# The last tile of a fused attention and two-MoE kernel: order of the gated half-groups on TensorE, and where the expert weights' conversions and the row-number copies stand on VectorE

## The chip, the cores and the metric

The kernel runs on one core of a Trainium2 chip. The metric is the device time of one execution in microseconds (us). The page of the profile and the trace come from one execution of the kernel taken by the hardware profiler; the times are those of runs of the same kernel.

## What is computed

Three layers follow one another. `q`, `k`, `v` are 2 x 8 x 576 x 64, so there are N = 1152 tokens of width 512.

```python
# attention with the 32 largest scores of each row kept
scores = q @ k.T / sqrt(64); kth = 32nd largest of the row
attn = softmax(where(scores >= kth, scores, -1e9)); x = attn @ v        # -> (1152, 512)
# first MoE layer: RMS norm, gate, value, output (d_ff = 1536)
xn = x / rms(x) * rms_g
g = xn @ w_gate;  x = (silu(g) * (xn @ w_val)) @ w_out
# second MoE layer: every token goes to the expert with the largest logit (8 experts, F = 1024)
e = argmax(x @ r_gate); gate = softmax(x @ r_gate)[e]
disp[e, counts[e]] = x[token]            # at most `capacity` = 288 tokens an expert
out[token] = gate * (relu(disp[e] @ w1[e]) @ w2[e])[pos]
```

## The kernel before

The tokens are cut into nine tiles of 128 (NT = 9, the last is tile 8). All products of the two MoE layers use numbers split into two 16-bit halves ("high" and "low"), so one product of float32 numbers is three matmuls: high x high, high x low, low x high.

**The first layer of a tile** is `moe1` (L479). The 1536 columns are worked on in three groups g = 0, 1, 2 of 512. A group has two half-groups, the gate (w = 0) and the value (w = 1), numbered b = 2g + w, so b runs from 0 to 5. A half-group is 12 matmuls (four chunks of the contraction by three) into one bank of PSUM (L500). After the gate half, ScalarE takes tanh (L507) and VectorE makes `th = (th + 1) * a` (L508); after the value half, VectorE makes `gs = a * vg * th` (L511). `turned` (L483) transposes the result with four TensorE transposes (L486), and `halves` (L469) splits it into `hT`: ScalarE copies the high half (L470), VectorE subtracts for the low one (L471). The output product is 36 matmuls, f = 0 to 11 by three (L528), which read `hT` of group f // 4; ScalarE evicts it as `yx` (L532).

For the last tile, four of the six half-groups write banks of the pool `late`, which has two buffers (`if late and b % 3`: b = 1, 2, 4, 5); b = 0 and 3 write a bank of `pm`. So b = 4 can only start when `gs` of group 0 has read b = 1.

**The dispatch of a tile** (L537 and following) transposes `yx` (L541), takes the router's logits (L555), splits the row into halves, finds the largest logit and the token's position, writes the slot (L616) and scatters the row with an indirect DMA issued by GpSimd to the buffer `disp` (L618). In the last tile its small steps are VectorE's; in the others many are GpSimd's. In the last tile's dispatch the first 128 tokens of expert 0 are fetched by a transposing DMA on SP (`gather("a", ...)`, L838), which waits for the scatter of tile 7; the remaining tokens of expert 0 come after the last scatter, by an indirect DMA on GpSimd into `xb` (L899) and a transposing DMA on SP into `xbT` (L903).

**The experts' weights** are 16 matrices of 2 MB in the order `ORDER = [0, 1, 2, 3, 4, 6, 5, ...]` (2e is w1 of expert e, 2e + 1 is w2). Each is loaded in two pieces on SP's queue (L776), `size` takes its sum of squares on ScalarE (L792) and works out a power of two as its scale in some small VectorE steps (L801 to L813, L148, L151) around a small TensorE sum (L803), and `convert` makes its halves. For the first four weights `convert` works in four pieces of 128 x 1024: high of pieces 0 and 1 on ScalarE (L822), high of pieces 2 and 3 on VectorE (L824), low of all four on VectorE (L827). The later ones are worked on in two pieces of 128 x 2048.

**The expert products** are `up` (L916 into `acc`; then L927 on ScalarE and L928 on VectorE make `hE`) and `down` (L916; then L936 on VectorE makes `yT`). "a" is the first 128 tokens of expert 0, "b" its other 48, then come experts 1 to 7 with room for 168 tokens each. `send` transposes, scales and scatters the result to the rows whose numbers `target` (L940) has copied into integers (L944 for "a" and "b", L948 for the others, L974 in `finish`).

**What sets the order.** The program is written as generators that are advanced by hand; each engine's queue is then put in order by the compiler's scheduler, which simulates the engines and takes instructions that are ready by priority. An engine runs its queue strictly in that order. `with after(t, name):` puts every instruction traced in the block behind the named one if both run on the same engine, and nothing else. Before the change such orders stand at these places: the first output matmuls of the last tile (f = 0, 1) behind the transposes of group 1, the others behind those of group 2 (L526); weight 0 and 1's conversion behind the split of `xn` of tile 8 ("xn"), weight 2's behind the split of the last tile's last `hT` ("dve"), and weight 3's behind the last tile's slot ("slot"):

```python
    with after(NT - 1, "xn"):
        convert(0, 0)
    size(2, 2)
    with after(NT - 1, "xn"):
        convert(1, 1)
    with after(NT - 1, "dve"):
        convert(2, 2)
    ...
    up("a", 0, WA, 2)
    with after(NT - 1, "slot"):
        convert(3, 3)
```

Of the kernel before, what the change touches and what calls it, by code (L numbers as in the profile page):

```python
# [62 lines left out]
def whole(  # L63
# [371 lines left out]
    def norm(t, ew):  # L435
# [30 lines left out]
        behind[t, "xn"] = halves(xnT[t], xn)  # L466
        yield

    def halves(out, x):  # L469
        nc.scalar.activation(out[:, :KC], x, AF.Copy)  # L470
        return nc.vector.tensor_tensor(out[:, KC:], x, out[:, :KC], op=OP.subtract)  # L471
# [7 lines left out]
    def moe1(t, ew):  # L479
# [10 lines left out]
        for g in range(3):  # L490
# [3 lines left out]
            for w in range(2):  # L494
                b = 2 * g + w
                a = late[0].tile([P, DM], F32, name="late") if late and b % 3 else pm.tile([P, DM], F32, name="pm")
                for c in range(KC):
                    i = KC * b + c
                    for n, (x, lo) in enumerate(((0, 0), (0, 1), (KC, 0))):
                        nc.tensor.matmul(a, xn[:, x + c, :], half(i, lo), start=(c == 0 and n == 0), stop=(c == KC - 1 and n == 2))  # L500
# [5 lines left out]
                if w == 0 and ew is nc.vector:  # L506
                    nc.scalar.activation(th, a, AF.Tanh, scale=gdec[:, g:g + 1])  # L507
                    nc.vector.scalar_tensor_tensor(th, th, 1.0, a, op0=OP.add, op1=OP.mult)  # L508
                elif ew is nc.vector:
                    h = mx.tile([P, DM], F32, name="x" if t == NT - 1 and g == 1 else "gs")  # L510
                    nc.vector.scalar_tensor_tensor(h, a, vg[:, g:g + 1], th, op0=OP.mult, op1=OP.mult)  # L511
# [10 lines left out]
        for f in range(NF1):  # L522
# [3 lines left out]
            with after(t, "turn", 1 if f < 2 else 2) if t == NT - 1 else nullcontext():  # L526
# [10 lines left out]
    def dispatch(t):  # L537
# [69 lines left out]
        ev.tensor_scalar(yd[:, DM:DM + 1], nm[:, 3:4], yn[:, 2:3], 1.0 / YS, op0=OP.mult, op1=OP.mult)  # L607
# [207 lines left out]
    def convert(j, n):  # L815

        raw, (hi, lo), sc = raw_of(n), place(j), sized.pop(j)
        k = 4 if n < 4 else 2
        for g in range(k):
# [5 lines left out]
        for g in range(k):  # L825
            r = slice(g * 2 * BIG // k, (g + 1) * 2 * BIG // k)
            nc.vector.scalar_tensor_tensor(lo[:, r], raw[:, r], sc[:, 7:8], hi[:, r], op0=OP.mult, op1=OP.subtract)  # L827
# [48 lines left out]
    with after(NT - 1, "xn"):  # L876
        convert(0, 0)
    size(2, 2)
    with after(NT - 1, "xn"):
        convert(1, 1)  # L880
    with after(NT - 1, "dve"):
        convert(2, 2)
# [47 lines left out]
    def down(k, e, n):  # L930
        yT2[k] = eb.tile([P, KC, n], F32, name="yT2", bufs=1)
        for lo, hi in groups(KC, n):
# [3 lines left out]
            nc.vector.tensor_scalar(yT2[k][:, lo:hi, :], a, es[e][:, 8:9], None, op0=OP.mult)  # L936
# [28 lines left out]
    def finish():  # L965
# [36 lines left out]
    with after(NT - 1, "slot"):  # L1002
        convert(3, 3)
# [118 lines left out]
```

## Time and profile before

| what | value |
|---|---|
| time of three runs | 668.9 us median (666.94 to 671.46) |
| the profiled execution's own time | 668.38 us |
| its span, from the first to the last instruction | 666.2 us |
| TensorE busy in the span | 588.6 us (88%) |
| VectorE busy | 542.3 us (81%) |
| ScalarE busy | 502.6 us (75%) |
| GpSimd busy | 350.4 us (53%) |
| mean granted TensorE clock | 0.976 of full speed |

PE is TensorE's matmuls, PEld its weight loads, DVE is VectorE, ACT ScalarE, POOL GpSimd, SP SyncE, which issues most DMAs; PEclk is the granted TensorE clock as a share of the full 2.4 GHz. Times in the trace count from the span's start. In a timeline a row is a run of like instructions: start, time covered, engine, line, operation, output and inputs, shape, count, and in brackets how long the engine was idle before it and what ended that. Attention and the first eight tiles fill the time to about 487 us, the last tile's first layer the time to about 523 us, its dispatch that to about 529 us, and the experts the rest.

### The profile page before, as it was taken

Reading aid. Unit: us, or ns where it says so; the run is one execution under the profiler, and the core shown is the slowest. Engines: PE = TensorE matmul, PEld = TensorE weight load, DVE = VectorE, ACT = ScalarE, POOL = GpSimd, SP = SyncE. Lnnn points to the kernel's source line nnn. Section 1 sums busy time; section 2 is a strip of 40 time slices with the busy share of each in tenths; the row PEclk is TensorE's granted clock in tenths of the full one; section 3 lists DMA queues with packets and bytes.
Section 4 is the critical chain, followed back from the end, with each engine's and each line's share of the span. In section 5 each row is a group of like instructions: output and inputs, shape, how many; then the busy total and the mean of one; then the engine's idle time right before and its main releaser. Section 6 shows DMA issues by size and latency. Waiting matters only on the chain. (4 is left out here: it accounts for less than half of the span.)

```text
span 666.2 us, 13476 instructions
## 1 busy us (share of the span) xinstructions
PE 588.6 (88%) x4817; PEld 412.8 (62%) x4817; DVE 542.3 (81%) x1495; ACT 502.6 (75%) x972; POOL 350.4 (53%) x490
## 2 busy tenths in 40 slices
PE   1417879789999999999999999999998879999995
PEld 1304455445666666666666666665544679999995
DVE  3979999978989979989988999861476867999951
ACT  3359979897787978878897988885697429899711
POOL 2476735636368879958788698683212100121412
PEclk9999979899999999999999999999998879999998
DMA  7988445923100010100000000007500589999001
GB/s 214 260 294 294 179 139 183 322 84 89 33 14 27 18 44 9 33 17 29 13 16 27 17 26 0 1 17 293 213 16 1 174 237 372 344 356 305 33 22 42
DMA packets 47006, 80.05 MB, mean 120 GB/s; under 512 B 18716, under 2 KB 23324, under 8 KB 46930
## 3 DMA queue, kind: packets, MB, share of 16 engines
q1 hardware_dynamic: 45138, 74.28, 35.2%
q0 software_dynamic: 1792, 4.83, 2.2%
q8 instruction: 39, 0.64, 0.4%
q14 instruction: 37, 0.30, 0.1%
HBM read 64.35 MB, written 12.27 MB: 115 GB/s over the span
## 5 line engine op out<-in xcount | busy, mean ns | idle before, releaser
L500 PE MATMUL pm<-wbig,xn 128*128 128x512 f16 x600 | 147.9, 381 | 0.5 <-DVE hT L471 0.5
L916 PEld LDWEIGHTS <-split 128*128 128x128 f16 x1728 | 117.4, 100 | 5.7 <-issue 5.6
L399 POOL TENSOR_TENSOR pp<-s,pp 128x576 f32<-128x576 f32 x72 | 102.3, 1436 | 21.5 <-ACT pp L398 21.1
L500 PEld LDWEIGHTS <-xn 128*128 128x128 f16 x648 | 62.7, 99 | 64.1 <-issue 5.3
L376 DVE MAX8 m<-r 128x8 f32<-128x288 f32 x216 | 96.4, 451 | 2.5
L373 DVE MATCH_REPLACE8 r<-m,r 128x288 f32<-128x288 f32 x216 | 95.0, 441 | 0.0
L317 PE MATMUL tp<-kst,qh 128*128 128x288 f32 (+1 forms) x160 | 64.4, 410 | 33.9 <-ACT s L319 16.8
L528 PE MATMUL pm<-wbig,hT 128*128 128x512 f16 x324 | 76.7, 380 | 0.0
L827 DVE SCALAR_TENSOR_TENSOR split<-raw,sc,split 128x2048 f16<-128x2048 f32 (+1 forms) x32 | 65.6, 2078 | 0.7 <-ACT split L822 0.7
L319 ACT ACTIVATE s<-tp 128x288 f32<-128x288 f32 x144 | 56.8, 417 | 10.7 <-PE tp L317 8.9
L317 PEld LDWEIGHTS tp<-kst,qh 128*128 128x128 f32 (+1 forms) x160 | 31.1, 195 | 53.0 <-ACT s L319 23.7
L423 ACT ACTIVATE pt<-tp 128x384 f32<-128x384 f32 x108 | 51.9, 500 | 15.6 <-PE tp L422 11.1
L916 PE MATMUL acc<-hE,split 128*128 128x168 f16 (+2 forms) x864 | 60.9, 233 | 2.5 <-DVE hE L928 2.2
L430 PE MATMUL xps<-pt,vt 128*64 128x128 f32 (+1 forms) x800 | 62.4, 275 | 0.0
L422 PE MATMUL tp<-ident,pp 128*128 128x128 f32 x324 | 58.0, 288 | 4.9 <-DVE r L325 2.6
L792 ACT ACTIVATE junk<-raw 128x2048 bf16<-128x2048 f32 (+1 forms) x32 | 54.1, 1691 | 8.2 <-DMA raw<-in_w_dram 6.4
L916 PE MATMUL acc<-xgT,split 128*128 128x168 f16 (+1 forms) x768 | 58.1, 238 | 2.3 <-DVE yT L936 1.5
L398 ACT ACTIVATE pp<-s,bias 128x576 f32<-128x576 f32 x72 | 52.2, 777 | 9.3 <-POOL bias L381 9.2
L404 ACT ACTIVATE pp<-pp,bias 128x576 f32<-128x576 f32 x72 | 57.0, 792 | 2.3 <-POOL pp L399 2.1
L422 PEld LDWEIGHTS tp<-ident,pp 128*128 128x128 f32 x324 | 40.3, 145 | 23.7 <-DVE r L325 3.4
L430 PEld LDWEIGHTS xps<-pt,vt 128*64 128x64 f32 x800 | 43.9, 138 | 13.7 <-issue 11.6
L528 PEld LDWEIGHTS <-hT 128*128 128x128 f16 x324 | 30.0, 98 | 32.0 <-issue 1.0
(241 smaller groups left out, 1226.5 us busy)
## 6 DMA issues: line engine op xcount, KB each, us to landing
raw<-in_w_dram SPq DMA_DIRECT2D x28, 1024.0 KB, 8.1
wbig<-in_w_gate_dram SPq DMA_DIRECT2D x6, 1024.0 KB, 9.0
wbig<-in_w_val_dram SPq DMA_DIRECT2D x6, 1024.0 KB, 9.8
wraw<-in_w_out_dram SPq DMA_DIRECT2D x12, 512.0 KB, 6.1
disp<-wraw SPq DMA_DIRECT2D x18, 257.0 KB, 5.5
qraw<-in_q_l_dram SPq DMA_DIRECT2D x72, 64.0 KB, 2.2
wbig<-in_k_l_dram SPq DMA_DIRECT2D x16, 288.0 KB, 4.0
split<-in_w_dram SPq DMA_DIRECT2D x4, 1024.0 KB, 7.6
```

Source lines behind the costliest of these rows:

```text
L317: nc.tensor.matmul(sp[:c1], x[:, i, :c1], kst[b, hp][:, i, c * HALF:(c + 1) * HALF], start=(n == 0), stop=(n == 1))
L319: nc.scalar.activation(s[:, c * HALF:(c + 1) * HALF], sp, AF.Copy)
L373: nc.vector.match_replace(h[i], to[n - 1][:, i], h[i], -3.0e38)
L376: nc.vector.max(to[n][:, i], h[i])
L399: nc.gpsimd.tensor_tensor(w, s[i], w, op=OP.subtract)
L404: nc.scalar.activation(pp[p][:, i], pp[p][:, i], AF.Exp, bias=bias[:, i, 0:1], scale=0.125, accum_out=sums[t][:, h:h + 1])
L422: nc.tensor.transpose(tp[:, i, :], p2[:, o:o + P], ident)
L430: nc.tensor.matmul(xps[t][rows, hp, c0:c1], v, w, start=(n == 0), stop=(n == 4))
L500: nc.tensor.matmul(a, xn[:, x + c, :], half(i, lo), start=(c == 0 and n == 0), stop=(c == KC - 1 and n == 2))
L528: nc.tensor.matmul(yps, hT[f // KC][:, KC * hi + f % KC, :], half(i, lo), start=(f == 0 and n == 0), stop=(f == NF1 - 1 and n == 2))
L827: nc.vector.scalar_tensor_tensor(lo[:, r], raw[:, r], sc[:, 7:8], hi[:, r], op0=OP.mult, op1=OP.subtract)
L916: nc.tensor.matmul(a, u[:, c, col * P:(col + 1) * P], v[:, c, :a.shape[-1]], start=(c == 0 and n == 0), stop=(c == nk - 1 and n == 2))
```

## The change

Five things are changed, all of them orders.

1. In the last tile, half-group b = 1 is put behind all products of b = 0, b = 3 behind all four transposes of group 0, b = 5 behind those of group 1. The output products f = 0, 1 stand behind b = 5 instead of behind group 1's transposes.
2. `convert` can be called for its high halves and for some of its low pieces alone.
3. Weight 1: high, and low of pieces 0 and 1, as before; low of 2 and 3 behind `gs` of group 0. Weight 2: high behind `th` of group 1 (its ScalarE part behind that group's tanh), low of 0 and 1 behind `gs` of group 1, low of 2 and 3 behind the last `hT` split ("dve").
4. Weight 3: high, and low of 0 and 1, behind "dve" (ScalarE: behind tanh of group 2) instead of behind the slot; low of 2 and 3 stay behind the slot (and behind the gate value written in the dispatch).
5. The row-number copies (L944, L948, L974) are put behind the `yT` of the same part ("a", "b"), those of the other experts behind the `yT` of "b".

Weight 0's conversion is also put behind the ScalarE half of the `xn` split; it stood behind it already.

```diff
@@ moe1
+                ahead_of = (None, ("prod", 0), None, ("turn", 0), None, ("turn", 1))[b] if t == NT - 1 else None
...
-                    for n, (x, lo) in enumerate(((0, 0), (0, 1), (KC, 0))):
-                        nc.tensor.matmul(a, xn[:, x + c, :], half(i, lo), start=(c == 0 and n == 0), stop=(c == KC - 1 and n == 2))
+                    with after(t, *ahead_of) if ahead_of else nullcontext():
+                        for n, (x, lo) in enumerate(((0, 0), (0, 1), (KC, 0))):
+                            behind[t, "prod", b] = nc.tensor.matmul(
+                                a, xn[:, x + c, :], half(i, lo), start=(c == 0 and n == 0), stop=(c == KC - 1 and n == 2))
...
-            with after(t, "turn", 1 if f < 2 else 2) if t == NT - 1 else nullcontext():
+            with after(t, *(("prod", 5) if f < 2 else ("turn", 2))) if t == NT - 1 else nullcontext():
@@ convert
-    def convert(j, n):
+    def convert(j, n, high=True, low=range(4)):
...
-        for g in range(k):
+        for g in range(k) if high else ():
...
-        for g in range(k):
+        for g in low[:k]:
@@ the calls
-    with after(NT - 1, "xn"):
+    with after(NT - 1, "xn"), after(NT - 1, "xn high"):
         convert(0, 0)
     size(2, 2)
     with after(NT - 1, "xn"):
-        convert(1, 1)
+        convert(1, 1, True, (0, 1))
+    with after(NT - 1, "gs", 0):
+        convert(1, 1, False, (2, 3))
+    with after(NT - 1, "th", 1), after(NT - 1, "tanh", 1):
+        convert(2, 2, True, ())
+    with after(NT - 1, "gs", 1):
+        convert(2, 2, False, (0, 1))
     with after(NT - 1, "dve"):
-        convert(2, 2)
+        convert(2, 2, False, (2, 3))
...
-    with after(NT - 1, "slot"):
-        convert(3, 3)
+    with after(NT - 1, "dve"), after(NT - 1, "tanh", 2):
+        convert(3, 3, True, (0, 1))
+    with after(NT - 1, "slot"), after(NT - 1, "gate"):
+        convert(3, 3, False, (2, 3))
@@ target, finish
-            nc.vector.tensor_copy(to[:m], meta[k, i][:m, 1:2])
+            with after(k, "down"):
+                nc.vector.tensor_copy(to[:m], meta[k, i][:m, 1:2])
...
-            nc.vector.tensor_copy(targets[i][:m, 1:], every[i][:m, 1:, 1])
+            with after("b", "down"):
+                nc.vector.tensor_copy(targets[i][:m, 1:], every[i][:m, 1:, 1])
...
-            nc.vector.tensor_copy(to[:m], every[i][:m, k, 1:2])
+            with after("b", "down"):
+                nc.vector.tensor_copy(to[:m], every[i][:m, k, 1:2])
```

## Rows read from the trace of the kernel before

**Rows 1.** Busy time by stretch: engines, PEclk, DMA share, GB/s.
```profile
487.00:498.10 11.10, 11.10 (x63) 5.38 (x61) 9.86 (x23) 11.01 (x20) 0.69 (x2) 1.00 0.00 0
498.10:501.65 3.55, 0.23 (x7) 0.16 (x5) 3.55 (x7) 3.55 (x7) 0.43 (x1) 1.00 0.01 2
501.65:505.40 3.75, 3.75 (x12) 1.86 (x12) 3.58 (x11) 3.72 (x8) 0.00 (x0) 0.54 0.01 4
...
515.65:522.80 7.15, 7.10 (x34) 3.27 (x34) 5.86 (x7) 0.61 (x2) 1.36 (x2) 1.00 0.40 83
...
527.94:533.60 5.66, 5.66 (x75) 5.66 (x75) 5.62 (x14) 4.33 (x5) 1.98 (x3) 0.70 0.18 67
533.60:538.80 5.20, 1.69 (x19) 1.34 (x17) 2.88 (x9) 0.60 (x1) 1.06 (x1) 0.72 0.88 149
...
555.00:640.00 85.00, 82.96 (x1195) 82.17 (x1193) 82.28 (x132) 71.86 (x77) 15.54 (x9) 1.00 0.80 252
```

**Rows 2.** Timeline of PE in the last tile's first layer.
```profile
487.08 0.59 PE L500 MATMUL pm<-wbig,xn 128*128 128x512 f16 x2
...
493.98 3.83 PE L500 MATMUL late<-wbig,xn 128*128 128x512 f16 x17
...
501.65 1.33 PE L500 MATMUL late<-wbig,xn 128*128 128x512 f16 x3 [3.32 <-DVE gs L511]
...
515.65 0.63 PE L486 MATMUL pm<-ident,gs 128*128 128x128 f32 x4 [1.26 <-DVE gs L511]
516.11 6.64 PE L528 MATMUL pm<-wbig,hT 128*128 128x512 f16 x30
```

**Rows 3.** Timeline of DVE in the last tile.
```profile
497.80 0.68 DVE L508 SCALAR_TENSOR_TENSOR th<-th,pm 128x512 f32<-128x512 f32 x1
498.40 2.47 DVE L827 SCALAR_TENSOR_TENSOR split<-split,sc,split 128x1024 f16<-128x1024 f32 x2
...
500.85 0.74 DVE L511 SCALAR_TENSOR_TENSOR gs<-late,st,th 128x512 f32<-128x512 f32 x1
...
517.55 1.41 DVE L824 TENSOR_SCALAR split<-raw,sc 128x1024 f16<-128x1024 f32 x2
518.87 4.87 DVE L827 SCALAR_TENSOR_TENSOR split<-raw,sc,split 128x1024 f16<-128x1024 f32 x4
...
524.26 0.15 DVE L562 TENSOR_SCALAR yn<-yn 128x1 f32<-128x1 f32 x1 [0.46 <-ACT th L549]
```

**Rows 4.** Timeline of ACT: the tanh of the last tile's group 1.
```profile
502.81 0.67 ACT L507 ACTIVATE th<-late,st 128x512 f32<-128x512 f32 x1
```

**Rows 5.** Timelines of PE, DVE, ACT and SP around the last slot; last row: landing of xbT.
```profile
524.02 1.50 PE L916 MATMUL acc<-xgT,split 128*128 128x128 f16 x24
...
538.79 6.67 PE L916 MATMUL acc<-hE,split 128*128 128x128 f16 x83 [1.77 <-DVE hE L928]
...
528.63 0.27 DVE L616 TENSOR_SCALAR slot<-pos 128x1 int32<-128x1 f32 x1
...
530.14 4.87 DVE L827 SCALAR_TENSOR_TENSOR split<-raw,sc,split 128x1024 f16<-128x1024 f32 x4
...
538.00 0.14 DVE L944 CAST to<-xb 48x1 int32<-48x1 f32 x1 [2.31 <-DMA xb<-disp,rest]
...
531.72 0.58 ACT L927 ACTIVATE hE<-acc 128x512 f16<-128x512 f32 x1
...
537.99 1.19 SPq L903 DMA_TRANSPOSE xbT<-xb  x1
...
DMA to landing us min/median/max: 2.7/2.7/2.7
```

**Rows 6.** Timelines of POOL and SP: the scatters of tiles 7 and 8, gather "a".
```profile
515.39 1.12 POOL L618 DMA_INDIRECT disp<-yd,slot  x1 [0.33 <-POOL slot L616]
...
529.77 1.39 POOL L618 DMA_INDIRECT disp<-yd,slot  x1 [1.40 <-ACT junk L792]
...
518.45 1.36 SPq L838 DMA_TRANSPOSE xgT<-disp  x1
```

More of the change, by code (lines that the diff above doesn't have):

```diff
@@ L465, in norm, with halves @@
             nc.tensor.transpose(xn[:, c, :], sq[:, c * P:(c + 1) * P], ident)
-        behind[t, "xn"] = halves(xnT[t], xn)
+        behind[t, "xn"] = halves(xnT[t], xn, t, "xn high")
         yield
-    def halves(out, x):
-        nc.scalar.activation(out[:, :KC], x, AF.Copy)
+    def halves(out, x, *what):
+        behind[what] = nc.scalar.activation(out[:, :KC], x, AF.Copy)
         return nc.vector.tensor_tensor(out[:, KC:], x, out[:, :KC], op=OP.subtract)
@@ L506, in moe1 @@
                 if w == 0 and ew is nc.vector:
-                    nc.scalar.activation(th, a, AF.Tanh, scale=gdec[:, g:g + 1])
-                    nc.vector.scalar_tensor_tensor(th, th, 1.0, a, op0=OP.add, op1=OP.mult)
+                    behind[t, "tanh", g] = nc.scalar.activation(th, a, AF.Tanh, scale=gdec[:, g:g + 1])
+                    behind[t, "th", g] = nc.vector.scalar_tensor_tensor(th, th, 1.0, a, op0=OP.add, op1=OP.mult)
                 elif ew is nc.vector:
                     h = mx.tile([P, DM], F32, name="x" if t == NT - 1 and g == 1 else "gs")
-                    nc.vector.scalar_tensor_tensor(h, a, vg[:, g:g + 1], th, op0=OP.mult, op1=OP.mult)
+                    behind[t, "gs", g] = nc.vector.scalar_tensor_tensor(h, a, vg[:, g:g + 1], th, op0=OP.mult, op1=OP.mult)
                 elif w == 0:
@@ L606, in dispatch @@
         ev.tensor_scalar(pos[:, 2:3], pos[:, 0:1], float(cap), NOWHERE, op0=OP.is_ge, op1=OP.mult)
-        ev.tensor_scalar(yd[:, DM:DM + 1], nm[:, 3:4], yn[:, 2:3], 1.0 / YS, op0=OP.mult, op1=OP.mult)
+        behind[t, "gate"] = ev.tensor_scalar(yd[:, DM:DM + 1], nm[:, 3:4], yn[:, 2:3], 1.0 / YS, op0=OP.mult, op1=OP.mult)
         yield
@@ L813, in scale @@
             nc.vector.tensor_tensor(es[e][:, 8:9], es[e][:, 4:5], sc[:, 4:5], op=OP.mult)
-    def convert(j, n):
-        raw, (hi, lo), sc = raw_of(n), place(j), sized.pop(j)
+    def convert(j, n, high=True, low=range(4)):
+        raw, (hi, lo), sc = raw_of(n), place(j), sized[j]
         k = 4 if n < 4 else 2
-        for g in range(k):
+        for g in range(k) if high else ():
             r = slice(g * 2 * BIG // k, (g + 1) * 2 * BIG // k)
@@ L935, in down @@
                 product(a[:, c - lo, :], place(2 * e + 1), hE[k], NF2, DM, c)
-            nc.vector.tensor_scalar(yT2[k][:, lo:hi, :], a, es[e][:, 8:9], None, op0=OP.mult)
+            behind[k, "down"] = nc.vector.tensor_scalar(yT2[k][:, lo:hi, :], a, es[e][:, 8:9], None, op0=OP.mult)
     targets = {}
```

## The prediction

> **What bounds the kernel now.** I read first the busy time by stretch, to find where TensorE stands idle or runs slowly, then the timelines of the four engines there, to find who was late.
>
> The busy times show two regimes. Over the experts, from 555 to 640 us, TensorE is busy for 82.96 of 85 us and VectorE for 82.28 [rows 1]: two engines without room, so that stage is moved as a whole by what happens before it, and neither can run ahead of the other for long. The last tile is different. TensorE is full up to 498.1 us, then does 0.23 us of work in 3.55 us, and then runs for 3.75 us at a granted clock of 0.54, the lower of its two levels for nearly all of it [rows 1]. A second hole of 1.26 us stands before the last four transposes [rows 2]. After the last slot it happens a third time: in the 5.2 us from 533.6 TensorE works 1.69, so 3.51 are lost, at a clock of 0.72 [rows 1].
>
> Who was late is read from the brackets. Both holes of the tile wait for `gs` (L511) [rows 2]. VectorE was not waiting for data in front of the first: `th` ends at 498.48, two low pieces of weight 1 follow (2.47 us), and only then comes `gs`, at 500.85 [rows 3], though TensorE had written its input by 495.1 (17 products from 493.98, the first five of b = 1, at 0.215 us; the rate is 30 products in 6.64 - 0.19 us) [rows 2]. The hole after the slot has two owners: weight 3's conversion, whose low pieces hold VectorE from 530.14 to 535.01, and the row-number copy of "b", which stops VectorE 2.31 us for a DMA, with the second `hE` behind it [rows 5].
>
> **The change part by part.**
>
> *Half-groups in turn.* No matmul is added. The first thirteen places of the tile now alternate b = 0 and b = 1; given to b = 0 alone, its twelve end near 487.08 + 12 x 0.215 = 489.7 instead of 494.0 [rows 2]. So tanh and `th` can come up to 4 us earlier, between weight 0's pieces, and `gs` may stand where `th` stood, at 497.8 [rows 3]; its input is there since 495.1. It then ends near 498.5, and TensorE's hole shrinks from 3.32 to about 0.5. With so short a hole I take the clock as not falling: after the hole of 1.26 us the row from 515.65 shows 1.00 [rows 1]. That gives back 3.75 x (1 - 0.54) = 1.7 us too. Recoverable, with the second hole, is 3.32 + 1.7 + 1.26 = 6.3 us.
>
> I don't take all of it, since a new wait appears. TensorE, from 498.6, has four transposes (0.45), b = 3 and b = 4 (24 x 0.215 = 5.2) before group 1's transposes, so it gets there soon after 504. These need `gs` of group 1, hence tanh of group 1, which ScalarE does at 502.81 [rows 4]; ScalarE is full (11.01 of 11.10 us [rows 1]) and the change takes nothing from it before that. Then `th` (0.68), the two high pieces of weight 2 that are now allowed behind it (1.41) and `gs` (0.75) follow, with hand-overs: near 507.0. Then 0.45 of transposes and b = 5 (2.6) to 510.0, f = 0, 1 (1.3) to 511.3, while `gs` of group 2 needs about 0.95 after b = 5: no hole. The last transposes start near 511.3 instead of 515.65 [rows 2]: **4.3 us earlier**, so 2.0 of the 6.3 are given back. Below, if `gs` keeps its place behind weight 1's pieces, only the second hole and some of the slow stretch go (1.7); above, nothing is given back (6.3).
>
> *Conversions between the gates.* VectorE gets no more work in sum. Behind "dve" it had 1.41 + 4.87 = 6.28 us of weight 2 [rows 3]; it will have 2.47 of weight 2 and 1.41 + 2.47 of weight 3, 6.35. This lies beside the 30 output products (6.64) and was over just before the dispatch's first step at 524.26 [rows 3]: I cost it at nothing. Without that cover it would be late by what is left of it. On ScalarE the two high pieces of weight 3 fall into a stretch in which it works 0.61 of 7.15 us [rows 1].
>
> *After the slot.* There VectorE had 6.3 us of weight 3 and now has 2.47, so from 528.9 it is free near 531.4. The first high `hE` is ready at 531.72 + 0.58 [rows 5], so the first low one ends near 533, and the second near 535. TensorE, which comes to `down("a")` at 533.6, then finds 12 products and hardly a hole (0.4). Of the 3.51 us lost, 3.1 return. The clock is 0.70 from 527.94 and 0.72 from 533.6 [rows 1]; without the hole `down("a")` should run nearer full speed. Its 83 products take 6.67 us, 0.080 each, against 0.0625 in the row of like ones from 524.02 (24 in 1.50) [rows 5]: worth up to 1.4. So `down("a")` would end 4.5 earlier than now, at 541.0 instead of 545.5, all before the shift of the tile is counted; `up("b")` needs `xbT`, issued at 537.99 with 2.7 to landing [rows 5], so 540.7: just there. That lead is no gain in time yet: VectorE is busy 82.28 of the 85 us that follow [rows 1] and has 2.7 us of holes to catch up with, and TensorE's own queue holds the sums for the weights' scales (L803), which need VectorE's steps first. The ends are 0 and 4.5; I take the middle, **2.2 us**, which lies within what VectorE's holes allow.
>
> *The copies behind `yT`* cost nothing: the scatters that need them come after the eviction of the same part's results.
>
> *Sum.* 4.3 + 2.2 = 6.5 us. The profiled execution took 668.38 (span 666.2, and 2.2 around it), 0.5 below the median of the runs: 668.4 - 6.5 = **661.9 us**.
>
> **The rivals.**
>
> *Stall kept (22%).* VectorE's order is made by a scheduler that had two low pieces between `th` and `gs` [rows 3] although the input was there; `convert(1)` keeps those two pieces free to stay in front. Then 1.7 + 2.2 = 3.9: 664.5. Against it: `th` itself moves up.
>
> *Nothing passed on after the slot (12%).* VectorE sets the pace over the experts and the TensorE lead is waited away: 668.4 - 4.3 = 664.1. For it speaks 82.28 of 85.
>
> *Slower (11%).* Weight 3's pieces, now free before the slot, are put between the small dependent steps of the last dispatch, which the scheduler does elsewhere (the pieces between `th` and `gs`). Six pieces are at hand, 6.35 us. If all land there, the slot (528.63 [rows 5]) is late by 6.3; with the first stall kept (1.7) the sum is +4.6, less 2.2 later: 668.4 + 2.4 = 670.8. It turns slower than before once more than 3.9 us of them stand in that chain. Against it: weight 2's 6.28 us ended before 524.26 in the same place.
>
> *Everything (9%).* Nothing is given back and the experts take the whole lead: 6.3 + 4.5 = 10.8: 657.6.
>
> *Tile 7's scatter late (6%).* Its steps on GpSimd now run beside conversions on VectorE. Gather "a" waits for this scatter (518.45), and TensorE uses it at 524.02 [rows 5, 6], in front of the dispatch's logits; the cover is at most 5.57 - 2.7 = 2.9 (by the landing of `xbT`), say 1.5. Three steps held by a piece of 1.22 each would be 3.7, so 2.2 too late: 668.4 - 4.3 = 664.1.
>
> On this the last scatter's row speaks: it took 1.39 us where tile 7's took 1.12 [rows 6], and high pieces of weight 3 ran on VectorE beside it. The Trainium skill (SBUF — State Buffer, "Who interferes with whom") says that the two engines share a port pair, that a scaling of this kind holds it for the whole instruction and that an instruction with two SBUF inputs holds off GpSimd's reads. The longer scatter agrees. By that rule tile 7's routing would meet the pieces now placed there and this rival would be likelier; the row alone shows 0.27 us.
>
> **How the numbers follow.** The forecast has 40%. About what a measurement can tell from no change is 1%, here 6.7 us, so faster means below 662.2 and slower above 675.6. The forecast lies just inside the first, so some six tenths of its share count there (24), with all of "everything" (9) and a part of the three near 664 (10): 0.43. Slower by over 1% needs all of the slow rival and more: 0.05. The rest, 0.52, is within. The range 657 to 668.5 takes in the forecast, the three at 664 and half of the upper end; it leaves out most of the slow rival.
>
> **What would show it.** Right: tanh of group 0 before 493 us; no hole over 1 us at the first group's transposes, and a clock of 1.00 there; a hole of about 2 us before group 1's transposes; the last transposes near 511.3; the slot near 524.3; no hole over 0.5 us at the start of `down("a")`; VectorE as full as before over the experts. Wrong: two low pieces still in front of `gs`, a conversion inside the dispatch's chain, or a TensorE wait for the scale sums (L803) that takes back the lead.

## The result, and the profile after

| | before | after |
|---|---|---|
| time, median of seven runs each on one chip | 669.5 us (666.94 to 671.46) | 662.4 us (660.06 to 663.67) |
| ratio, with its 95% interval | | 0.990 (0.987 to 0.992) |
| the profiled execution's own time | 668.38 us | 663.15 us |
| its span | 666.2 us | 661.2 us |
| mean granted TensorE clock | 0.976 | 0.976 |

The forecast of 661.9 us is 0.5 from the median. The time was right; of the two terms that made it, one came to half of its size, the other to nothing, and a third that I had not named made up for them. That their sum came out so near the forecast is luck. The rest of the document is about that.

Of the 5.2 us between the two profiled executions, 2.4 lie ahead of the last tile: its first product starts at 487.08 before and at 484.72 after. In both kernels the instructions of each engine stand in the same order up to there, and in the profiles of this study that start lies anywhere from 482.8 to 487.1. So times in the tile are compared from its own first product, and I call that t0.

Line numbers from L500 to L822 have moved by two or three and those from L916 by nine to eleven: L502 is the half-groups' products, L510, L511 and L514 tanh, `th` and `gs`, L531 the output products, L806 the scale sums, L825, L827 and L830 the conversions (high on ScalarE, high on VectorE, low), L925 the experts' products, L936 and L937 `hE`, L945 `yT`. In the kernels of the experiments the lines from L916 on differ from these by a few more.

The busy time by stretch, as in [rows 1], for the kernel after:

```profile
core 0: us, PE busy (x) PEld busy (x) DVE busy (x) ACT busy (x) POOL busy (x), PEclk, DMA share, GB/s
484.70:495.80 11.10, 11.10 (x62) 5.44 (x61) 9.97 (x23) 11.04 (x21) 0.90 (x2) 1.00 0.00 0
495.80:499.30 3.50, 3.50 (x24) 1.88 (x23) 3.50 (x9) 3.50 (x5) 0.05 (x1) 1.00 0.02 5
499.30:503.00 3.70, 3.09 (x19) 1.91 (x17) 3.70 (x7) 3.70 (x9) 0.00 (x0) 1.00 0.00 0
503.00:510.80 7.80, 5.43 (x33) 3.08 (x34) 7.80 (x22) 4.11 (x10) 3.47 (x5) 0.98 0.04 6
510.80:518.90 8.10, 8.06 (x30) 3.10 (x28) 7.35 (x13) 2.72 (x4) 3.92 (x5) 0.81 0.54 190
...
549.80:554.40 4.60, 4.53 (x112) 4.50 (x112) 4.23 (x15) 4.60 (x6) 0.00 (x0) 0.68 1.04 415
...
555.00:640.00 85.00, 83.77 (x1144) 83.20 (x1142) 81.18 (x133) 70.89 (x77) 16.72 (x10) 1.00 0.74 237
```

The second row answers to the hole of [rows 1]: TensorE worked 0.23 of 3.55 us there and now works all of 3.50, and the stretch at 0.54 behind it is gone. But the fourth row has 2.37 idle us in 7.80, the fifth runs at 0.81, and near 550 there is a stretch at 0.68 that the kernel before doesn't have. Where the idle time went is read from the brackets of the timelines. TensorE after, against [rows 2]:

```profile
496.36 0.60 PE L486 MATMUL pm<-ident,gs 128*128 128x128 f32 x4
...
503.55 0.66 PE L486 MATMUL pm<-ident,x 128*128 128x128 f32 x4 [1.16 <-DVE x L514]
...
510.04 0.72 PE L486 MATMUL pm<-ident,gs 128*128 128x128 f32 x4 [1.82 <-DVE gs L514]
510.55 8.31 PE L531 MATMUL pm<-wbig,hT 128*128 128x512 f16 x30
...
531.26 4.79 PE L925 MATMUL acc<-hE,split 128*128 128x128 f16 x83 [0.51 <-DVE hE L937]
537.74 2.60 PE L925 MATMUL acc<-xbT,split 128*128 128x48 f16 x96 [1.68 <-DMA xbT<-xb]
...
549.87 0.19 PE L806 MATMUL st<-s,ones 128*128 128x1 bf16 x2 [2.94 <-DVE s L804]
```

The first group's transposes wait for nothing. Those of group 1 wait 1.16, those of group 2 wait 1.82 (1.26 in [rows 2]), and the 30 output products behind them take 8.31 us instead of 6.64, in this execution. In the other two profiles of the changed kernel they take 6.64. In the second profile TensorE ran slowly earlier, behind the wait of 1.16, and so met the last `gs` without a hole. In all three the last transposes start 25.3 us after t0: it is `gs` that sets their time. VectorE after, against [rows 3], tells why:

```profile
493.96 0.75 DVE L514 SCALAR_TENSOR_TENSOR gs<-late,st,th 128x512 f32<-128x512 f32 x1
...
496.54 2.46 DVE L830 SCALAR_TENSOR_TENSOR split<-split,sc,split 128x1024 f16<-128x1024 f32 x2
...
499.05 2.46 DVE L830 SCALAR_TENSOR_TENSOR split<-split,sc,split 128x1024 f16<-128x1024 f32 x2
...
501.50 0.67 DVE L511 SCALAR_TENSOR_TENSOR th<-th,late 128x512 f32<-128x512 f32 x1
...
503.81 1.08 DVE L588 SCALAR_TENSOR_TENSOR key<-lg,m,rank 128x8 f32<-128x8 f32 x1
...
506.86 2.46 DVE L830 SCALAR_TENSOR_TENSOR split<-raw,sc,split 128x1024 f16<-128x1024 f32 x2
509.25 0.73 DVE L514 SCALAR_TENSOR_TENSOR gs<-late,st,th 128x512 f32<-128x512 f32 x1
...
512.03 1.28 DVE L830 SCALAR_TENSOR_TENSOR split<-raw,sc,split 128x1024 f16<-128x1024 f32 x1
...
513.29 1.27 DVE L830 SCALAR_TENSOR_TENSOR split<-raw,sc,split 128x1024 f16<-128x1024 f32 x1
...
549.65 0.17 DVE L804 CAST s<-sc 128x2 bf16<-128x2 f32 x1 [8.20 <-ACT junk L795]
```

Group 0 has its `gs` before any piece of weight 1. Group 1's `th` stands behind two low pieces of weight 1 (499.05), group 2's `gs` behind two low pieces of weight 2 (506.86). The stall of the kernel before has not left; it has gone two groups on.

To see where the time comes from over all profiles I cut each into four stretches at marks that every trace has: t0, the last four transposes of `moe1` (L486), the last slot (L619), the first product of the third expert, and the last matmul's end. For the kernel before these are 487.08, 515.65, 528.63, 557.65 and 659.33, for the changed one 484.72, 510.04, 524.74, 554.36 and 654.61. The differences, in us:

| kernel | t0 to last transposes | to the slot | to the third expert | to the end |
|---|---|---|---|---|
| before, two profiles | 28.57, 28.57 | 12.98, 12.98 | 29.02, 29.24 | 101.68, 104.34 |
| after, three profiles | 25.32, 25.34, 25.33 | 14.70, 13.66, 13.56 | 29.62, 29.31, 28.98 | 100.25, 99.50, 100.62 |
| order alone | 23.36 | 12.99 | 32.33 | 100.39 |
| conversions alone | 23.55 | 17.48 | 29.44 | 99.77 |
| copies alone | 27.40 | 12.99 | 32.24 | 101.04 |
| order, weight 1, copies | 23.36 | 12.99 | 31.70 | 102.43 |
| after, weight 2's low pieces later | 23.37 | 17.98 | 26.60 | 101.98 |
| after, sixth weight loaded early | 25.32 | 15.80 | 28.97 | 101.88 |

Some expectations below name 22.6 us to the last transposes, or 40.6 us to the slot. They count the order alone and the kernel with weight 2's pieces later from the tile's fourth product, 0.75 us behind the first; the table counts every kernel from its first.

In the mean over the profiles of each, the tile with its dispatch (the first two columns) gives 41.55 - 39.30 = 2.2 us, the way from the slot to the third expert gives nothing (29.13 against 29.30), and the rest of the experts gives 103.0 - 100.1 = 2.9. Together that is 5.0. The medians are 7.1 apart; the profiled executions of before took 668.38 and 667.45 us, both under their median of 669.5, which is most of the rest.

### The profile page after: what moved, and what is told of

The parts are those of the page before. It is cut to its first block, busy times and chain, and to the rows that moved or that the text cites. A ratio compares the mean times of both kernels' runs of the same rounds, so it can differ in the third digit from the quotient of the medians.

```text
span 661.2 us, 13479 instructions
## 1 busy us (share of the span) xinstructions
PE 588.5 (89%) x4817; PEld 412.1 (62%) x4817; DVE 540.5 (82%) x1495; ACT 502.3 (76%) x972; POOL 353.8 (54%) x490
## 4 chain that ended last, share of the span: by engine, by line
PE 52%; DVE 17%; ACT 9%; DMA 8%; POOL 6%; issue 6%; SPq 1%; POOLq 0%; DVEq 0%; ACTq 0%
PE pm L502 15%; PE pm L531 9%; PE acc L925 7%; PE xps L430 6%; PE tp L317 5%; PE tp L422 4%; DVE split L830 3%; DMA vt<-in_v_l_dram 3%; DMA raw<-in_w_dram 3%; ACT junk L795 2%; DVE r L373 2%; DVE wbig L169 2%; DVE wbig L168 2%; PE pm L486 2%; DVE split L827 2%
## 5 line engine op out<-in xcount | busy, mean ns | idle before, releaser
L502 PE MATMUL pm<-wbig,xn 128*128 128x512 f16 x600 | 145.7, 379 | 0.5 <-DVE hT L471 0.5
L925 PEld LDWEIGHTS <-split 128*128 128x128 f16 x1728 | 116.4, 99 | 4.3 <-issue 2.0
L502 PEld LDWEIGHTS <-xn 128*128 128x128 f16 x648 | 62.3, 98 | 60.2 <-issue 0.9
L531 PE MATMUL pm<-wbig,hT 128*128 128x512 f16 x324 | 78.4, 386 | 0.0
L830 DVE SCALAR_TENSOR_TENSOR split<-raw,sc,split 128x2048 f16<-128x2048 f32 (+1 forms) x32 | 65.9, 2077 | 0.5 <-ACT split L825 0.5
L925 PE MATMUL acc<-hE,split 128*128 128x168 f16 (+2 forms) x864 | 59.9, 231 | 1.7 <-DVE hE L937 1.7
L925 PE MATMUL acc<-xgT,split 128*128 128x168 f16 (+1 forms) x768 | 58.0, 239 | 0.0
L531 PEld LDWEIGHTS <-hT 128*128 128x128 f16 x324 | 30.4, 99 | 33.5 <-issue 2.7
```

The source lines that it names most:

```text
L502: behind[t, "prod", b] = nc.tensor.matmul(a, xn[:, x + c, :], half(i, lo), start=(c == 0 and n == 0), stop=(c == KC - 1 and n == 2))
L531: nc.tensor.matmul(yps, hT[f // KC][:, KC * hi + f % KC, :], half(i, lo), start=(f == 0 and n == 0), stop=(f == NF1 - 1 and n == 2))
L925: nc.tensor.matmul(a, u[:, c, col * P:(col + 1) * P], v[:, c, :a.shape[-1]], start=(c == 0 and n == 0), stop=(c == nk - 1 and n == 2))
```

## The experiments

Each kernel was compared with the kernel before on the same chip.

**1. The parts one by one, and the two kernels again.** For the order alone the calls of `convert` and the copies are put back:

```diff
-        convert(1, 1, True, (0, 1))
-    with after(NT - 1, "gs", 0):
-        convert(1, 1, False, (2, 3))
-    with after(NT - 1, "th", 1), after(NT - 1, "tanh", 1):
-        convert(2, 2, True, ())
-    with after(NT - 1, "gs", 1):
-        convert(2, 2, False, (0, 1))
+        convert(1, 1)
     with after(NT - 1, "dve"):
-        convert(2, 2, False, (2, 3))
+        convert(2, 2)
...
-    with after(NT - 1, "dve"), after(NT - 1, "tanh", 2):
-        convert(3, 3, True, (0, 1))
-    with after(NT - 1, "slot"), after(NT - 1, "gate"):
-        convert(3, 3, False, (2, 3))
+    with after(NT - 1, "slot"):
+        convert(3, 3)
```

For the conversions alone, the order (`ahead_of = None`, and f = 0, 1 behind the transposes of group 1 again) and the copies are put back; for the copies alone, the order and the conversions.

Order alone:

> Only part 1: the half-groups in turn, transposes in fours, f = 0, 1 behind b = 5. Conversions and copies as before. Theory T (the tile's gain is what reaches the end; the lead made after the slot is waited away at the weights' scale sums): gs of group 0 comes ahead of weight 1's low pieces, no hole over 1 us before group 0's transposes, none before the last transposes either since no low piece of weight 2 stands in front of gs of group 2, slot 4 to 6 us earlier counted from the tile's first matmul; the holes after the slot stay (3.5 us); ratio 0.991 to 0.995, so 663.5 to 666. Rival R (what counts is the room after the slot): the ratio is 0.996 to 1.000.

Conversions alone:

> Only parts 2 to 4: the weights' pieces placed around the gates and half of weight 3 ahead of the slot; half-groups and copies as before. Theory T: the first hole shrinks by the 2.5 us of the two low pieces that no longer stand in front of gs of group 0, conversions now stand in the last dispatch or in front of gs of group 2 and give some of it back; slot 0 to 3 us earlier; after the slot the row-number copy still stops VectorE for about 2 us; ratio 0.995 to 1.000. Rival R (room after the slot is what counts): 0.990 to 0.994.

Copies alone:

> Only part 5: the row-number copies behind the yT of the same part; everything else as before. Theory T: the second hE no longer waits for the DMA of xb, the TensorE hole of 1.8 us in down(a) goes, the lead of 2 us is waited away before 560 us: ratio 0.997 to 1.000. Rival R (the lead is kept): 0.995 to 0.997, about 2 to 3 us.

The changed kernel, and the kernel before, once more:

> The changed kernel once more, for a second profile. The first one began its last tile 2.4 us earlier than the kernel before although every queue is the same up to there. If that is the run and not the change, the start of the last tile here lies 0 to 3 us away from 484.7 and the distance from the tile's first matmul to the slot is 40.0 +- 0.3 (41.5 before), and the ratio is again 0.987 to 0.992. If it is the change, the last tile begins at 484.7 +- 0.5 again.

> The kernel before once more, for a second profile of it. Its first profile began the last tile at 487.1, the five other profiles between 483.6 and 486.5 although the queues up to there are the same. If that spread is the execution's and not the kernel's, the tile begins here anywhere from 483 to 487, the distance from its first matmul to the slot is 41.5 +- 0.5, and that from the first matmul to the last transposed result (172.3 before) is 171 to 174.

| kernel | median | ratio, interval |
|---|---|---|
| order alone | 663.96 us | 0.9934 (0.9911 to 0.9957) |
| conversions alone | 663.53 us | 0.9924 (0.9897 to 0.9951) |
| copies alone | 667.76 us | 0.9993 (0.9975 to 1.0012) |
| the changed kernel again | 661.34 us | 0.9907 (0.9874 to 0.994) |

The single run of the kernel before took 667.45 us. The order and the conversions are each worth about 0.7% by themselves, the copies nothing that can be measured. Added they would be 1.4%; the whole change gives 0.9 to 1.2% in its three measurements. With the intervals of these ratios that difference is not clear of noise, but the traces show that the two parts fill the same idle time: up to the last transposes the order alone gains 28.57 - 23.36 = 5.2 us and the conversions alone 28.57 - 23.55 = 5.0, of the 6.3 that the prediction called recoverable there. The order alone, TensorE at its first product, then VectorE, then TensorE:

```profile
482.81 0.81 PE L502 MATMUL pm<-wbig,xn 128*128 128x512 f16 x3
```

```profile
492.06 0.75 DVE L514 SCALAR_TENSOR_TENSOR gs<-late,st,th 128x512 f32<-128x512 f32 x1
...
494.63 2.46 DVE L830 SCALAR_TENSOR_TENSOR split<-split,sc,split 128x1024 f16<-128x1024 f32 x2
```

```profile
506.17 0.64 PE L486 MATMUL pm<-ident,gs 128*128 128x128 f32 x4
506.64 6.64 PE L531 MATMUL pm<-wbig,hT 128*128 128x512 f16 x30
...
545.07 0.19 PE L806 MATMUL st<-s,ones 128*128 128x1 bf16 x2 [4.68 <-DVE s L804]
```

With weight 1's conversion where it always was, `gs` of group 0 still goes ahead of its low pieces: the order of the products is enough for that. No piece of weight 2 stands in front of the last `gs`, the last transposes have no bracket, the output products take 6.64 again, and the slot is 36.35 us after t0, 5.20 earlier than before. Then more than half of it goes: TensorE waits 4.68 us for a scale sum, and the stretch to the third expert is 3.2 longer than before.

With the conversions alone the tile is quick too, 23.55 to the last transposes, but the dispatch takes 17.48 instead of 12.98. Up to the third expert this profile gains next to nothing, 70.47 us from t0 against 70.57 and 70.79 before. What the conversions gain in the median is not in these stretches; it may lie in the last one, which single profiles can't settle. GpSimd in that kernel, and below it TensorE:

```profile
512.63 1.28 POOL L620 TENSOR_TENSOR cum<-cum,oh 128x8 bf16<-128x8 bf16 x1 [0.90 <-PE px L599]
...
515.62 1.42 POOL L619 TENSOR_SCALAR slot<-pos 128x1 int32<-128x1 f32 x1
517.33 1.93 POOL L621 DMA_INDIRECT disp<-yd,slot  x1 [0.29 <-POOL slot L619]
```

```profile
524.34 2.72 PE L925 MATMUL acc<-xgT,split 128*128 128x128 f16 x24 [3.16 <-DMA xgT<-disp]
```

These are the routing steps and the scatter of tile 7. In the kernel before the same three took 0.20, 0.38 and 1.12 us; here pieces of the conversions run on VectorE beside them: two low ones from 512.59, two high ones from 515.59, two low ones from 516.99 to 519.46. The step at 515.62 ends at 517.04, the high pieces beside it at 517.01. The scatter is late, so gather "a" is late, and TensorE stands 3.16 us at the two columns of `up("a")`, which are in its queue in front of the last dispatch's sums. This is the rival to which I gave 6%. In the changed kernel the wait is there in small or not at all (0.80, 0.70, none), where the order has brought the scatter forward: it starts 27.5 us after t0 instead of 30.8.

**2. The sixth weight's load.** The scale sum that stops TensorE belongs to the second matrix of the third expert. SP issues its load only behind the last gathers. In the changed kernel, SP and then ScalarE:

```profile
536.14 1.46 SPq L841 DMA_TRANSPOSE xgT<-disp  x1
537.71 12.36 SPq L779 DMA_DIRECT2D raw<-in_w_dram  x8
```

```profile
543.76 1.91 ACT L795 ACTIVATE junk<-raw 128x2048 bf16<-128x2048 f32 x1 [2.90 <-DMA raw<-in_w_dram]
...
547.61 1.91 ACT L795 ACTIVATE junk<-raw 128x2048 bf16<-128x2048 f32 x1 [1.28 <-DMA raw<-in_w_dram]
```

The load is issued at 537.71, lands in two pieces 6.0 and 9.9 us later, ScalarE squares them, and VectorE, idle for 8.20 us, makes `s` at 549.65. To try whether this is what holds TensorE, the load goes ahead of the gathers, in the changed kernel and in one with the order and the copies alone:

```diff
+    fetch_w()
     last = gather(1, 1, 0, W, eb, nc.sync)
     rest_gather()
...
-        for _ in range(3):
+        for _ in range(2):
             fetch_w()
```

> The changed kernel with one more edit: the sixth weight (number 5 in the order of loading) is fetched ahead of the gathers of experts 1 to 3 on SP's queue, behind the conversion of weight 3 that frees its buffer, instead of behind them. Theory S (the lead of some 4 us that TensorE has after down(a) is lost because TensorE's queue holds the sum for this weight's scale, and the weight's load is issued only behind the last gather): TensorE's hole of 2.8 us before that sum goes, up(2) starts 3 us or more earlier counted from the tile's first matmul, VectorE uses its idle 8 us before it, and 2 to 4 us of it reach the end: ratio 0.984 to 0.988. Rival V (VectorE, busy 97% over the experts, sets the pace): the hole goes and others of the same sum come behind it; ratio 0.988 to 0.991, as the changed kernel.

> Parts 1 and 5 of the change and the early fetch of weight 5; weights 1 to 3 are converted as before the change (weight 2 behind the last hT, weight 3 behind the slot). Theory S: order alone brought the slot 6 us earlier and lost most of it at a hole of 4.7 us before the scale's sum; with the load early this hole shrinks to under 1.5 and the ratio is 0.981 to 0.987. Rival V: VectorE has half of weight 3 more to do behind the slot, so nothing is won on the changed kernel: 0.988 to 0.993.

Measured: 665.01 us, 0.9949 (0.9917 to 0.998), and 665.82 us, 0.9939 (0.9918 to 0.996), both by their medians slower than the changed kernel. The wait for the scale sum goes, and others come. TensorE in the changed kernel with the early load:

```profile
540.38 2.60 PE L925 MATMUL acc<-xbT,split 128*128 128x48 f16 x96 [2.55 <-DMA xbT<-xb]
...
552.41 0.19 PE L806 MATMUL st<-s,ones 128*128 128x1 bf16 x2 [0.67 <-DVE s L804]
```

2.94 has become 0.67, but `xbT` is waited for 2.55, where the three profiles of the changed kernel have 1.68, 1.38 and 1.37: SP issues its gather 12.0 us after the slot instead of 9.2 to 9.6. With the order and the copies that wait is 1.72, where the order alone has 0.41. The load was the cause of the wait for the scale sum, as expected; that moving it would pay was wrong. The weight and the gathers share SP's queue and the same stretch, and in these runs whichever was first made the other late. Gather "a" is waited for 1.06 us, little more than the 0.80 and 0.70 that the changed kernel has without the early load, but behind it TensorE ran at a granted clock of 0.51 for 6.17 us, and the slot came 15.80 us after the last transposes.

**3. Weight 2's low pieces out of the last gate's way.**

```diff
-    with after(NT - 1, "gs", 1):
+    with after(NT - 1, "gs", 2):
         convert(2, 2, False, (0, 1))
```

> The changed kernel with the first two low pieces of weight 2 behind gs of group 2 instead of group 1. If these pieces are what delays gs of group 2 and, beside tile 7's steps on GpSimd, its scatter: the last transposes start within 25 us of the tile's first matmul (25.3 in both profiles of the changed kernel, 22.6 with the order alone) by 1.5 us or more, GpSimd's scatter of tile 7 takes 1.1 to 1.4 us instead of 2.0, and the ratio is 0.986 to 0.990. If the lead is waited away at the weights' scale all the same: the slot is 1 to 2.5 us earlier and the ratio as before this edit, 0.989 to 0.991.

Measured: 665.17 us, 0.9939 (0.9906 to 0.9973), by its median slower than the changed kernel, though the intervals overlap. The tile did what was expected: 23.37 us to the last transposes, as with the order alone. In the changed kernel these pieces cost 25.33 - 23.37 = 1.96 us there. The dispatch then took 17.98. ScalarE and TensorE there:

```profile
512.68 2.19 ACT L825 ACTIVATE split<-raw,sc 128x1024 f16<-128x1024 f32 x2 [5.17 <-DVE sc L148]
514.78 0.67 ACT L535 ACTIVATE yx<-pm,st 128x512 f32<-128x512 f32 x1
```

```profile
515.50 0.66 PE L544 MATMUL px<-ident,yx 128*128 128x128 f32 x4 [2.14 <-ACT yx L535]
...
521.03 2.72 PE L925 MATMUL acc<-xgT,split 128*128 128x128 f16 x24 [2.68 <-DMA xgT<-disp]
```

The low pieces now hold up the small steps of weight 3's scale on VectorE; ScalarE idles 5.17 us for that scale (its bracket), and then its two high pieces stand in front of the last normalisation (L535). And the pieces again run beside tile 7's routing: its steps L620 and L619 took 1.27 and 1.45 us and its scatter 1.45, a little over the 1.1 to 1.4 expected. Gather "a" is waited for 2.68 us. The pieces were in the way in both places.

**4. Nothing of `up("a")` ahead of the last dispatch's sums.** With it, the changed kernel a third time.

```diff
-    up("a", 0, WA, 2)
+    up("a", 0, WA, 0)
```

> The changed kernel once more, as the reference for the two runs beside it: 661 to 663 us, ratio to the kernel before 0.988 to 0.992; slot numbers 39 to 40 us after the last tile's first product; weight 2's two low pieces in front of the gating of group 2 as before, third expert's up product 29 to 30 us after the slot.

> Weight 2's first low pieces behind the gating of group 2, and none of the first product of expert 1's first rows ahead of the last tile's dispatch sums. Theory (that product stands in TensorE's queue in front of the last dispatch sums and waits 2.7 us for its gather, which GpSimd's stretched scatter makes late): the last transposes stay 22.6 us after the tile's first product, the slot numbers come 36 to 37.5 us after it instead of 40.6, and the last gather and the sixth weight's load with them; the third expert's product 2 to 3 us earlier against the tile's start, 661.5 to 663 us, ratio 0.988 to 0.992. Rival (the product's 24 matmuls cost as much behind the dispatch as their wait did ahead of it, and the end is set by weights): slot earlier as above, but the third expert's product stays 66 to 68 us after the tile's start, ratio 0.993 to 0.996 as with the pieces moved alone.

> The changed kernel with none of the first product of expert 1's first rows ahead of the last dispatch sums. If the late gather is what ate the order's gain in the changed kernel, the slot numbers come 2 us or more earlier against the tile's first product (39 to 40 now) and the ratio falls below 0.988; if it was the low pieces in front of the last gating alone, the slot numbers come 1 us earlier at most, the 24 matmuls (1.3 us) stand behind them, and the ratio stays at 0.989 to 0.993.

Measured: the changed kernel 661.92 us, 0.9883 (0.9859 to 0.9907); with the pieces moved and this edit 674.08 us, 1.0065 (1.0041 to 1.0088); the changed kernel with this edit 671.43 us, 1.0023 (0.9995 to 1.0051). Both theories missed. With the pieces moved, the slot came at 38.92 us after t0 instead of 41.35; in the changed kernel at 40.01, inside what it has without the edit (38.9 to 40.0). But the scheduler, given another place for 24 products, wrote the experts' queues anew. TensorE in the second of the two:

```profile
531.84 0.22 PE L925 MATMUL acc<-hE,split 128*128 128x128 f16 x1
536.95 1.10 PE L925 MATMUL acc<-xbT,split 128*128 128x48 f16 x23 [4.90 <-DMA xbT<-xb]
537.88 6.28 PE L925 MATMUL acc<-hE,split 128*128 128x128 f16 x83
```

A first column of `up("b")` now stands in the middle of `down("a")`, and TensorE waits 4.90 us for its gather with 83 ready products behind it. What the edit by itself would be worth these two runs don't tell.

**5. Order, copies and weight 1 alone.** Weight 1 keeps its split around the first gate; weights 2 and 3 are converted where the kernel before has them.

> The order, the copies and the split of weight 1's low pieces around the first gating; weights 2 and 3 converted where the kernel before has them. Theory (the pieces of weights 2 and 3 are what takes the order's gain in the tile back, by standing in front of the last gating, of the last normalisation on ScalarE and beside tile 7's scatter): last transposes 22.5 to 23 us and slot numbers 35.5 to 36.5 us after the last tile's first product (25.3 and 39 to 40 in the changed kernel), tile 7's scatter 1.1 to 1.4 us on GpSimd instead of 2. What that is worth at the end: if the lead at the slot numbers is lost at the sixth weight's scale again, the third expert's product stays 31 to 33 us behind them and the time is that of the order alone, 663 to 665 us, ratio 0.991 to 0.995; if the earlier weights help behind it, 0.985 to 0.990 and it beats the changed kernel.

Measured: 663.82 us, 0.9922 (0.9896 to 0.9948). Last transposes at 23.36 us and the slot at 36.35, both as with the order alone, and tile 7's scatter 1.10 us, as the theory wanted; TensorE then waits 3.97 us for the sixth weight's scale sum, the third expert comes 31.7 after the slot, and the time is that of the order alone. The split of weight 1 adds nothing to the order. None of the kernels tried is faster than the changed one.

## Why the prediction was right, and where only its sum was

**Half-groups in turn.** The mechanism stood: tanh of group 0 is at 490.80 (forecast: before 493), `gs` at 493.96, the hole of 3.32 and the slow stretch behind it are gone. The term of 4.3 us was mis-sized in both directions. Alone, the order gave 28.57 - 23.36 = 5.21, which is nearly the 6.3 that I had called recoverable less the new wait of 1.16. The wait that I put before group 1's transposes came, 1.16 instead of 2.0 us, but not for my reason: ScalarE does that tanh at 498.79, well in time, and it is two low pieces of weight 1 in front of `th` (499.05) that make it late. In the whole change the tile gave 3.2 up to the last transposes (28.57 - 25.33), and with the slower output products and the dispatch 1.5 to 2.7 up to the slot. That the clock does not fall behind a short hole held in part: behind the wait of 1.16 it was 1.00 in two profiles of the changed kernel and 0.65 over 4.84 us in the other.

**Conversions between the gates, "I cost it at nothing".** This is the step that failed. I followed the pieces that lie beside the output products and put no price on the two low pieces of weight 2 that may stand between `gs` of groups 1 and 2. They stood directly in front of the latter: 2.46 us, hence a hole of 1.82 and, in the first profile, a clock of 0.81 behind it. Experiment 3 puts them at 1.96 us up to the last transposes, which is all that the changed kernel lacks there of the order alone. I had named this very trap for group 0 ("two low pieces between `th` and `gs`") and did not ask it again for the other groups.

**After the slot.** The first half stood: the hole in `down("a")` went from 3.51 us lost to 0.51, the 83 products take 4.79 instead of 6.67, and from the slot to `up("b")` it is 13.0 us (537.74 - 524.74) where it was 16.7. But I gave the hole two owners, and most of it belonged to one, the row-number copy. With the copies alone, weight 3's pieces all behind the slot as before, `up("b")` comes 13.2 us after the slot; with the conversions alone, the copy where it was, 17.1. TensorE with the copies alone, and VectorE with the conversions alone:

```profile
538.50 2.60 PE L919 MATMUL acc<-xbT,split 128*128 128x48 f16 x96 [0.65 <-DMA xbT<-xb]
```

```profile
536.99 0.15 DVE L953 CAST to<-xb 48x1 int32<-48x1 f32 x1 [6.12 <-DMA xb<-disp,rest]
```

The order alone has 12.9 too, since the scheduler there wrote the second `hE` ahead of the copy. The second half, that 2.2 us of that lead is passed on, was wrong: the third expert comes as late after the slot as before. The lead ends at the sixth weight's scale sum. Its load starts behind the last gathers, that is 12 to 13 us after the slot in either kernel, and the sum can't be taken before some 25 us after the slot (549.87 - 524.74 here). In the kernel before TensorE came to it just then and did not wait; now it comes 2.94 earlier, waits, and runs at a granted clock of 0.68 for the next 4.60 us, which is 1.5 more: 4.4 of the 4.5 us of lead that I had worked out. The rival that nothing is passed on (12%) had the right result, but not the cause: VectorE, which I thought too full, was idle for 8.20 us. The cause was the last item of my list of what would make it wrong, a TensorE wait for the scale sums.

**The copies at nothing:** right for the time, 0.9993, and not for the path: they win 3.5 us after the slot (16.7 - 13.2), and the wait for the scale sum, 4.42 us with the copies alone, takes it back.

**What I did not forecast** is the third term, some 2.9 us over the rest of the experts, which brought the time back to the forecast. TensorE's waits of 0.3 us and more from the third expert on add up to 2.9 and 5.2 us in the two profiles of before and to 1.7, 1.2 and 1.8 in the three of after. One of these waits is plain to see. In the kernel before, VectorE and then TensorE:

```profile
635.45 4.60 DVE L827 SCALAR_TENSOR_TENSOR split<-raw,sc,split 128x2048 f16<-128x2048 f32 x2
639.98 0.56 DVE L936 TENSOR_SCALAR yT<-acc,sc 128x336 f32<-128x336 f32 x1
```

```profile
640.59 1.90 PE L916 MATMUL acc<-xgT,split 128*128 128x168 f16 x24 [1.24 <-DVE yT L936]
```

and VectorE after:

```profile
630.76 0.56 DVE L945 TENSOR_SCALAR yT<-acc,sc 128x336 f32<-128x336 f32 x1
...
632.61 4.61 DVE L830 SCALAR_TENSOR_TENSOR split<-raw,sc,split 128x2048 f16<-128x2048 f32 x2
```

The last weight's two low pieces stood in front of a `yT` and now stand behind it. The hole of 1.25 is in both profiles of before, in the order alone, the copies alone and in the run with weight 1; it is in none of the kernels whose weights 2 and 3 are converted early, and not in the one with the order and the early load either. So it goes with how the scheduler writes VectorE's queue, which the change alters as a side effect. That this is the whole of the 2.9 us is not shown: single profiles of one kernel differ by as much there (101.68 and 104.34).

**The rivals.** The stall was not kept at its old place. The slower rival did not come: no piece stands in the last dispatch's chain in the changed kernel (it did when the low pieces were moved on, experiment 3). The late scatter of tile 7 was under-weighted: 3.16 and 2.68 us in two of the experiments, up to 0.80 in the changed kernel. And my best case of 657.6, that everything is recovered, asks for more than the tile of the order alone (5.2 of the 6.3) and needs the load to come earlier as well, which experiment 2 could not give it.

## What to carry to other kernels

When a filler is freed from one place of an in-order queue, ask at every following gate whether it now stands in front of that one; the stall here went from the first group to the third. A lead won on the bottleneck engine lasts only to the next thing that hangs on a clock of its own, here a load that is issued a fixed time after the last gather: look for the next wait whose releaser does not move with the lead before counting the lead as time. And two edits that each give 0.7% need not give 1.4% together, when both fill the same idle time.

## What the runs showed of the hardware

GpSimd's steps beside VectorE's conversions were longer than I expected. The step L620 took 0.20 us in the kernel before, 1.28 with the conversions alone and 1.02 in the changed kernel. GpSimd in the latter, to be laid beside the rows 506.86 and 512.03 of VectorE above:

```profile
508.37 1.02 POOL L620 TENSOR_TENSOR cum<-cum,oh 128x8 bf16<-128x8 bf16 x1 [1.33 <-PE px L599]
...
512.24 2.05 POOL L621 DMA_INDIRECT disp<-yd,slot  x1 [0.29 <-POOL slot L619]
```

508.37 + 1.02 is 509.39; the two low pieces from 506.86 on end at 509.32. The scatter, 1.12 us in [rows 6], took 2.05 from 512.24 on: what is left of the piece from 512.03 on, which ends at 513.31, is 1.07, and 0.98 behind it is nearly its own length. A further low piece, from 513.29 on, stood beside these 0.98, so a piece does not hold a scatter all the time that they overlap. In the second profile of the changed kernel L620 came 0.72 us behind the two pieces and took 0.20. The Trainium skill (SBUF — State Buffer, "Who interferes with whom") says that an instruction of VectorE with two inputs in SBUF, as a low piece has, contends with an instruction of GpSimd that reads SBUF, and that a scaling such as a high piece can take the pair of ports that the two engines share. The trace agrees for the small steps.

VectorE pays too. Its step L588 of 128x8 (503.81 above) took 1.08 us beside a step of GpSimd that ran from 503.70 to 504.86, and 0.22 in the kernel before, where no step of GpSimd ran beside it. With the order alone the scatter began 0.03 us behind the first of two high pieces and took 1.10; the two pieces took 1.63 instead of the 1.41 of [rows 3]:

```profile
508.08 1.63 DVE L827 TENSOR_SCALAR split<-raw,sc 128x1024 f16<-128x1024 f32 x2
```

The low pieces beside tile 7's scatter were no longer than elsewhere (1.28 and 1.27 in the changed kernel).

The other is the price of a short wait of TensorE. The same 96 products of `down("b")` took 2.58 us in the kernel before and 3.67 behind the wait of 2.94, at the granted clock of 0.68, between its two levels as a mean over the 4.60 us. In the other two profiles of the changed kernel the waits were 2.79 and 2.55, and the 4.6 us behind them ran at 0.65 and 0.68. With the copies alone the wait was 4.42 and the 6.7 us around and behind it ran at 0.65; in the kernel before the 5.0 us around the same scale sum had no wait and 1.00. A wait at this place cost here about half as much again as its bracket says. Elsewhere in the kernels the price did not follow the length. Copies alone, behind the same hole of 3.32 us that has a clock of 0.54 behind it in [rows 1], and the second profile of the changed kernel, behind the wait of 1.16:

```profile
500.22 0.81 PE L502 MATMUL pm<-wbig,xn 128*128 128x512 f16 x3
```

```profile
503.90 4.20 PE L502 MATMUL late<-wbig,xn 128*128 128x512 f16 x12
```

In the first the clock was 1.00 over the 3.75 us behind the hole, and that is why the copies alone reach the last transposes in 27.40 us instead of 28.57. In the second it was 0.65 over 4.84 us, and the twelve products took 4.20 us where the other two profiles have 2.75. What decides it these runs don't show.
